# Two more V tiles beside each chain are loaded as two halves

## The chip, the cores and the metric

The kernel runs on one core of a Trainium2 chip. The metric is the device time of one execution in microseconds (us), as the median of several runs; lower is better.

## The reference, cut to what matters

The program computes a decode step: 8 sequences (B), one token each (width D = 448), two layers of attention over a cached K and V, each followed by a small mixer and MLP block. Both layers use the same weights and the same cache.

```python
def _A_ref(x, k_cache, v_cache, wq, wo):          # B 8, Hq 16, Hkv 8, Sk 4096, Dh 256
    q = (x @ wq).reshape(B, Sq, Hq, Dh).transpose(0, 2, 1, 3)
    k = jnp.repeat(k_cache, 2, axis=1)
    v = jnp.repeat(v_cache, 2, axis=1)
    scores = jnp.einsum("bhqd,bhkd->bhqk", q, k) * (Dh ** -0.5)
    o = jnp.einsum("bhqk,bhkd->bhqd", _softmax(scores), v)
    return o.transpose(0, 2, 1, 3).reshape(B, Sq, Hq * Dh) @ wo

x = A_x
x = x + _A_ref(_layernorm(x), K, V, wq, wo)
x = x + _B_ref(_layernorm(x), w1, w2, w3, w4)     # ends in gelu(layernorm(x1) @ w3) @ w4
x = x + _A_ref(_layernorm(x), K, V, wq, wo)
x = x + _B_ref(_layernorm(x), w1, w2, w3, w4)
```

With one token, the shifts of the mixer move zeros in, so that the kernel needs only `w3` and `w4` of block B. K and V are 8 x 8 x 4096 x 256 values of bf16 each, 134 MB apiece; together, and twice, that is nearly all that the kernel reads.

## The kernel before, in words

**Tiles and tasks.** A task is one layer (`ps` 0 or 1), one sequence `b` and one of four pairs of K/V heads (`gp`). Its K and its V come in four tiles of 1 MB each, 128 partitions by 4096 values (8 KB a partition). A K tile is transposed in blocks by DVE (L779) and multiplied with the queries on PE (L794); ACT takes the exponential (L803). A V tile is multiplied with the probabilities on PE (`pv`, L847): 16 matmuls, each over 256 of the 4096 columns, in column order, with room for a step of other work between the eighth and the ninth where the caller asks for it. All tiles live in 15 places of SBUF (`places`, `slots`). Part of one sequence's tiles stay in their places from the first layer to the second and are not loaded again.

**The chain.** The second layer of a sequence can start only when its first layer is through all four pairs. That needs a string of small dependent steps, the chain: scale and turn the output (`half`, L477), multiply by `wo` (L365), normalise (L227 to L302, a sum over partitions on PE at L235, a power on POOL at L254), `w3` (L383), gelu, `w4` (L365), normalise again, `wq` (L316), and spread the query (L335, L339). There is one chain for each of the 8 sequences. The steps are Python generators; `step` lets them go on a little between the tiles, so that PE's instructions for a chain and those for V tiles alternate in one order that is fixed when the program is built.

**The order around a chain.** `first_kept` lays out the work of a sequence. The V tiles that are to be worked off beside the chain are collected in `due`: those of three or four tasks that were scored before. All of them go into `narrow`; for a narrow V, `pv` lets the chain step between its two halves of eight matmuls. Up to 11 of them (`AFTER`) are put directly behind the last V's of the sequence, and the rest are spread over what follows. In the text, "first V", "second V" and "third V" are `due[0]`, `due[1]` and `due[2]`, and their order on PE is that order.

**The loads.** SP issues all K and V loads, in the order in which the tiles are used (`emit_loads`), as soon as a place is free in that order. A place is free when PE or DVE has finished with what is in it. A tile in `halved` is loaded by two transfers of 512 KB (L769: columns 0 to 2047, then 2048 to 4095); any other by one of 1 MB (L766), and pairs of K tiles by one of 2 MB (L741). The matmuls of `pv` wait for the transfer that writes the columns which they read, and a transfer into a place waits for the matmuls that read the columns which it overwrites, so halves are waited for and released as halves. Beside a chain only three places take part: the first, second and third V have one each, the fourth uses the first V's, the fifth the second's, and so on.

Before the change, `halved` holds `due[2]` up to `due[n + 1]`, with `n` the number of V's put behind the last V's of the sequence (11, or 10 in the later chains). `due[0]` and `due[1]` are loaded whole.

Of the kernel before, what the change touches and what calls it, by code (L numbers as in the profile page):

```python
# [17 lines left out]
def kernel(  # L18
# [545 lines left out]
    tasks, items, due = [], [], []  # L564
    number, narrow, halved, loose = {}, set(), set(), set()
    AFTER = 11

    def block(k, v=None):

        fresh = [(number[v], 1, c) for c in range(4)] if v else []  # L570
        if k is None:
            due.extend(fresh)
            items.extend(due)
            due.clear()
            return
        number[k] = len(tasks)
        tasks.append(k)
        two = k[0] == 1 and k[2] in keep
        for c in range(4):
            items.append((number[k], 0, c))  # L580
            if two and c % 2 == 0:
                continue
            items.extend(due[:1])
            del due[:1]
            if c <= two:
                due.extend(fresh)

    def first_kept(b, units, before):

        k2, k3 = ((0, b, gp) for gp in keep)  # L590
        todo = list(units)
        block(todo.pop(0), before)
        if len(todo) > 2:
            block(todo.pop(0))
        block(k2)
        block(todo.pop(0), k2)
        if todo:
            block(todo.pop(0))
        assert not todo
        block(k3)  # L600
        block(None, k3)
        for u in units:
            due.extend((number[u], 1, c) for c in range(4))
        n = min(AFTER, len(due) - 2)
        narrow.update(due)
        if n == AFTER:
            loose.update(due)
        halved.update(due[2 : n + 2])
        items.extend(due[:n])
        del due[:n]  # L610

    block((0, 0, free[0]))
    block((0, 0, free[1]), (0, 0, free[0]))
    first_kept(0, ahead[0], (0, 0, free[1]))
    for b in range(Bn):
        k3, k2 = ((1, b, gp) for gp in keep[::-1])
        block(k3)
        block(k2, k3)
        if b + 1 < Bn:
            first_kept(b + 1, ahead[b + 1], k2)  # L620
        else:
            block((1, b, free[0]), k2)
            block((1, b, free[1]), (1, b, free[0]))
            block(None, (1, b, free[1]))
# [336 lines left out]
    for idx, it in enumerate(items):  # L961
# [7 lines left out]
        n, kv, c = it  # L969
# [202 lines left out]
```

## Time and profile before

| What | Value |
|---|---|
| Median of 3 runs | 1088.32 us (1086.39 to 1088.36) |
| The profiled execution | 1085.17 us, span 1083.3 us |
| Moved by DMA | 438.22 MB, mean 405 GB/s |
| K and V loads on SP | 65 of 2 MB, 62 + 123 of 1 MB, 170 of 512 KB, 8 of 768 KB |
| PE, DVE, ACT busy | 61%, 56%, 15% |

The profiled execution's own time stands beside its span: 1.87 us lie around the span. "L847" is a line of the kernel; `o<-places,ptw` names what an instruction writes and reads. PE is TensorE, PEld its weight loads, DVE VectorE, ACT ScalarE, POOL GpSimd; SPq is the sequencer of SyncE, which issues loads. "Landing" is the moment when the last part of a transfer has reported that it is done. The first row of loads for each chain stands in SP's timeline like this one, of the first chain (start, length from the first issue to the last, what, count):

```profile
149.50 32.45 SPq L769 DMA_DIRECT2D places<-in_A_v_cache_dram  x22
```

The eight chains begin with such rows at 149.50, 280.18, 409.48, 539.02, 657.43, 767.46, 877.55 and 988.17 us.

### The profile page before, as it was taken

To read this page: it belongs to the slowest core of one execution; us is meant where nothing else is said; L and a number is where in the kernel's file an instruction comes from. 1 tells how busy PE (TensorE), PEld (TensorE's weight loads), DVE (VectorE), ACT (ScalarE), POOL (GpSimd) and SP (SyncE) were. 2 spreads that over 40 slices of the span, in tenths; PEclk is the share of its full clock that TensorE was granted. 3 is DMA by queue.
4 is the path that set the end of the run, shared out by engine and by line. 5 is a ranking of instruction groups with operands and counts; after the bars stand their busy time and mean duration, and the time that the engine had idled before them with its cause. 6 is when DMAs were issued, how large, how long until landed. Compare 5 with 4: busy or idle time off the path is not lost.

```text
span 1083.3 us, 29794 instructions
## 1 busy us (share of the span) xinstructions
PE 655.5 (61%) x13292; PEld 411.6 (38%) x13292; DVE 610.5 (56%) x1266; ACT 161.9 (15%) x612; POOL 16.4 (2%) x27
## 2 busy tenths in 40 slices
PE   3244458644776447764486547754785468756775
PEld 2122235422443224532254324532453245433554
DVE  4357841677326872368625773297329743874271
ACT  0001111111111111111112111111111111111110
POOL 0000000000000000000000000000000000000000
PEclk9985555655565555655556555655566556655565
DMA  9999999999999999999999999999999999999994
GB/s 360 394 425 427 425 394 390 423 424 424 394 411 423 428 420 379 415 426 422 421 388 420 423 423 389 388 424 426 405 384 426 424 384 400 426 423 405 394 420 182
DMA packets 66896, 438.22 MB, mean 405 GB/s; under 512 B 7112, under 2 KB 11088, under 8 KB 34384
## 3 DMA queue, kind: packets, MB, share of 16 engines
q1 hardware_dynamic: 66576, 435.94, 98.4%
q8 instruction: 104, 1.70, 0.6%
q10 hardware_dynamic: 192, 0.38, 0.1%
q14 instruction: 24, 0.20, 0.0%
HBM read 436.28 MB, written 0.01 MB: 403 GB/s over the span
## 4 chain that ended last, share of the span: by engine, by line
DMA 60%; PE 19%; DVE 14%; SPq 3%; issue 2%; ACT 1%; POOL 1%; DVEq 0%; ACTq 0%
DMA places<-in_A_v_cache_dram 30%; DMA places<-in_A_k_cache_dram 29%; DVE places L779 9%; PE sc L794 6%; PE o L847 5%; PE misc L365 2%; SPq L174 2%; PE misc L383 1%; PE misc L316 1%; PE misc L477 1%; SPq L766 1%; DVE places L821 1%; DMA wq_sb<-in_A_wq_dram 1%; POOL t L254 1%; DVE qbd L339 1%
## 5 line engine op out<-in xcount | busy, mean ns | idle before, releaser
L779 DVE STREAM_TRANSPOSE places<-places 128x512 uint32<-128x512 uint32 (+1 forms) x576 | 458.0, 855 | 126.0 <-DMA places<-in_A_k_cache_dram 123.7
L794 PE MATMUL sc<-places,qbd 128*8 128x256 bf16 (+1 forms) x4896 | 246.9, 352 | 241.9 <-DVE places L779 234.4
L847 PE MATMUL o<-places,ptw 128*8 128x256 bf16 x3968 | 250.1, 387 | 114.2 <-DMA places<-in_A_v_cache_dram 93.2
L794 PEld LDWEIGHTS <-qbd 128*8 128x8 bf16 x4896 | 129.4, 104 | 324.6 <-DVE places L779 145.3
L847 PEld LDWEIGHTS <-ptw 128*8 128x8 bf16 x3968 | 101.0, 102 | 178.3 <-issue 96.1
L803 ACT ACTIVATE p_n<-sc 128x256 bf16<-128x256 f32 x128 | 95.0, 742 | 382.9 <-PE sc L794 382.9
L957 ACT COPY ptw<-psv 128x32 bf16<-128x32 bf16 x248 | 52.4, 225 | 202.3 <-PE o L847 187.2
L837 ACT CAST psv<-misc 128x128 bf16<-128x128 f32 x64 | 17.1, 267 | 233.7 <-PE misc L830 233.7
L441 DVE RECIPROCAL rz<-misc 128x8 f32<-128x8 f32 (+1 forms) x35 | 6.6, 189 | 70.2 <-PE misc L438 70.2
L316 PEld LDWEIGHTS <-wq_sb 128*128 128x128 bf16 x1152 | 34.2, 104 | 28.0 <-issue 18.1
L365 PEld LDWEIGHTS <-wo_sb 128*128 128x128 bf16 x1280 | 38.1, 103 | 16.4 <-issue 16.2
L339 DVE CAST qbd<-misc 32x64 bf16<-32x64 f32 x104 | 22.4, 215 | 30.9 <-PE misc L335 29.9
L477 PE MATMUL misc<-R_t,o_sb 128*128 128x8 f32 (+1 forms) x132 | 28.6, 326 | 13.4 <-ACT o_sb L471 7.1
L316 PE MATMUL misc<-xb,wq_sb 128*128 128x1 bf16 x1024 | 33.3, 166 | 4.5 <-issue 2.8
L477 PEld LDWEIGHTS misc<-R_t,o_sb 128*128 128x128 f32 x132 | 25.7, 272 | 24.4 <-ACT o_sb L471 14.0
L803 ACT ACTIVATION_READ_ACCUMULATOR p_n<-sc 128x1 f32 x128 | 33.5, 262 | 0.0
L365 PE MATMUL misc<-OT,wo_sb 128*128 128x1 bf16 x1024 | 31.8, 165 | 2.0 <-DVE OT L481 1.7
L473 DVE MEMSET o<- 128x256 f32 x33 | 9.0, 272 | 39.6 <-PE o L847 37.0
L325 DVE CAST qT<-misc 128x32 bf16<-128x32 f32 x8 | 1.5, 192 | 52.7 <-PE misc L316 52.7
L254 POOL TENSOR_TENSOR t<-t,nhalf 128x2 f32<-128x2 f32 (+2 forms) x20 | 14.0, 705 | 1054.7 <-DVE t L275 1054.7
L383 PE MATMUL misc<-xb,w_sb 128*128 128x1 bf16 (+1 forms) x560 | 19.1, 166 | 10.5 <-DVE xb L283 6.4
L383 PEld LDWEIGHTS <-w_sb 128*128 128x128 bf16 x560 | 18.1, 105 | 18.6 <-issue 17.8
(107 smaller groups left out, 306.9 us busy)
## 6 DMA issues: line engine op xcount, KB each, us to landing
places<-in_A_k_cache_dram SPq DMA_DIRECT2D x65, 2048.0 KB, 19.3
places<-in_A_v_cache_dram SPq DMA_DIRECT2D x123, 1024.0 KB, 21.1
places<-in_A_v_cache_dram SPq DMA_DIRECT2D x170, 512.0 KB, 6.7
places<-in_A_k_cache_dram SPq DMA_DIRECT2D x62, 1024.0 KB, 16.1
places<-in_A_v_cache_dram SPq DMA_DIRECT2D x8, 768.0 KB, 6.8
wo_sb<-in_A_wo_dram SPq DMA_DIRECT2D x1, 3584.0 KB, 27.5
wq_sb<-in_A_wq_dram SPq DMA_DIRECT2D x3, 1024.0 KB, 9.0
w_sb<-in_B_w_dram SPq DMA_DIRECT2D x1, 1568.0 KB
```

Source lines behind the costliest of these rows:

```text
L174: nc.sync.dma_start(t[:, fc * cols : (fc + 1) * cols], src[fc * 128 : fc * 128 + 128, :])
L254: nc.gpsimd.tensor_tensor(rs[:, k0:k1].rearrange("p n b -> p (n b)"), ve[:, k0:k1].rearrange("p n b -> p (n b)"), nhalf[:].to_broadcast([1 ...
L316: nc.tensor.matmul(q_ps[:, j * Hq + h, :], w, xbs(nb)[:, xi, :], start=(fc == 0), stop=(fc == 3),)
L339: nc.vector.tensor_copy(qbd[32 * a : 32 * a + 32, :, :, a, :], qs.rearrange("p e (f g u h) -> p (e f) u g h", f=2, u=2, h=2)[:, :, u],)
L365: nc.tensor.matmul(y_ps[:, fc, :], w[:, i, at : at + 128], rhs(i), start=start, stop=stop, skip_group_check=open is not None,)
L383: nc.tensor.matmul(h_ps[:, c * nb : c * nb + nb], w, xbs(nb)[:, xi, :], start=(fc == 0), stop=(fc == 3),)
L477: nc.tensor.matmul(ot_ps[:, j], o_sb[:].rearrange("p (i j) -> p j i", j=2)[:, j], R, start=True, stop=True)
L779: nc.vector.transpose(w, w)
L794: nc.tensor.matmul(sc[32 * k : 32 * k + 8, 128 * x : 128 * (x + nx)], qbd[:, ep, gp].rearrange("p a h -> p (a h)"), v, start=(n == 0), sto ...
L803: nc.scalar.activation(p_sb[:, :, :, 2 * u : 2 * u + 2].rearrange("p t i x -> p x t i"), sc[:, 256 * u : 256 * u + 256].rearrange("p (x t ...
L847: nc.tensor.matmul(o_ps[32 * q : 32 * q + 8, :], ptz[:, at : at + 8], v[:, y * Dh : (y + 1) * Dh], start=False, stop=(y >= 12), skip_group ...
L957: nc.scalar.copy(ptw[:, ring_of[it], :, 6:8], psv[slot_of[it[0]]][:, it[2]])
```

## The change

`halved` begins with `due[0]`: the first and the second V beside each chain are loaded as two transfers of 512 KB each, as the ones after them already are. Nothing else is changed. In the program's order of instructions, SP has 16 more transfers: before each of the eight chains, the last two of the whole V loads become four halves (22 halves in a row become 26 in the first four chains, 20 become 24 in the last four). PE, DVE, ACT and POOL have the same instructions in the same order.

```diff
@@ -605,7 +605,7 @@
         narrow.update(due)
         if n == AFTER:
             loose.update(due)
-        halved.update(due[2 : n + 2])
+        halved.update(due[: n + 2])
         items.extend(due[:n])
         del due[:n]
 
```

## The prediction

> **What bounds the kernel now.** I read the page's first lines, then the chain of work that ended last, then three stretches in the view by windows, then one chain step by step (V's and chains as named in the section on the kernel).
>
> From the page:
>
> ```profile
> PE 655.5 (61%) x13292; PEld 411.6 (38%) x13292; DVE 610.5 (56%) x1266; ACT 161.9 (15%) x612; POOL 16.4 (2%) x27
> ...
> q1 hardware_dynamic: 66576, 435.94, 98.4%
> q8 instruction: 104, 1.70, 0.6%
> ...
> DMA 60%; PE 19%; DVE 14%; SPq 3%; issue 2%; ACT 1%; POOL 1%; DVEq 0%; ACTq 0%
> ```
>
> No engine is over 61% busy; the load queue is at 98.4%, and 60% of the chain is DMA. The kernel is bound by loads, so a change counts if it lets the loads run closer to their full rate. By windows (length, busy of PE, PEld, DVE, ACT, POOL, granted clock, DMA share, GB/s), one stretch before and one inside each of the first two chains:
>
> ```profile
> 122.00:147.00 25.00, 10.93 (x212) 5.59 (x202) 19.70 (x25) 3.54 (x11) 0.00 (x0) 0.50 1.01 422
> 157.00:167.00 10.00, 8.76 (x196) 5.58 (x189) 2.69 (x16) 0.98 (x5) 0.71 (x1) 0.50 0.95 322
> 253.00:278.00 25.00, 10.18 (x196) 5.07 (x184) 19.70 (x25) 3.38 (x12) 0.00 (x0) 0.50 1.01 422
> 287.00:297.00 10.00, 9.02 (x216) 6.14 (x217) 2.62 (x15) 1.15 (x6) 0.70 (x1) 0.50 0.99 358
> ```
>
> Beside a chain the loads fall from 422 GB/s to 322 and 358. Why, the first chain shows. PE's timeline (start, length, what, idle time before it and what ended it):
>
> ```profile
> 152.73 1.03 PE L847 MATMUL o<-places,ptw 128*8 128x256 bf16 x16 [0.51 <-DMA places<-in_A_v_cache_dram]
> 155.31 0.60 PE L847 MATMUL o<-places,ptw 128*8 128x256 bf16 x8 [1.55 <-DMA places<-in_A_v_cache_dram]
> 155.84 1.02 PE L477 MATMUL misc<-R_t,o_sb 128*128 128x8 f32 x4
> 156.79 0.60 PE L847 MATMUL o<-places,ptw 128*8 128x256 bf16 x8
> ...
> 159.74 1.03 PE L847 MATMUL o<-places,ptw 128*8 128x256 bf16 x16
> 160.69 0.59 PE L235 MATMUL misc<-t,one 128*128 128x2 f32 x2
> 161.21 1.03 PE L847 MATMUL o<-places,ptw 128*8 128x256 bf16 x16
> ```
>
> The x8 at 155.31 is the first half of the first narrow V; it waited for the whole megabyte, though its eight matmuls read only the first 512 KB. The chain of waits has that load and a later one:
>
> ```profile
> 132.51 22.67 DMA places<-in_A_v_cache_dram
> 155.18 0.14 issue
> 155.31 0.60 PE o L847 x8
> 155.91 0.95 PE misc L477 x4
> ...
> 165.44 0.56 PE o L847 x8
> 166.00 0.02 issue
> 166.02 7.69 DMA places<-in_A_v_cache_dram
> ```
>
> The first narrow V lands at 132.51 + 22.67 = 155.18. The loads behind it wait for PE to free a place: SP issues the third V's halves at 149.50 and 149.93, then nothing until the first V's halves are used, at 155.95 and 157.44. Six microseconds without an issue, with about 3 MB in the queue at 150, run the queue low, and 157 to 167 is where the rate falls. In total PE waits for V loads:
>
> ```profile
> PE o L847 <- DMA places<-in_A_v_cache_dram: 93.2, 72, 6.1
> ```
>
> **The change, part by part.** The order of instructions on PE, DVE, ACT and POOL does not move. On SP, two whole V loads (L766) before each of eight chains become four halves (L769): 16 more transfers, no more bytes.
>
> *Removed: the wait of the first narrow V.* Halves in line land 1.25 us apart (the third V's at 158.91 and 160.16), so the first half of the first V should land at about 153.95 instead of 155.18. PE ends the V before at 153.76, so it starts at about 154.07: 1.24 earlier. In the eight chains the wait there is 1.55, 1.00, 1.03, 1.44, 1.15, 1.40, 1.56 and 0.98; capped at 1.24 that is 9.1 us. What is late next in chain 1: L477, whose operand ACT has ready at 154.2, then the second half, landing at 155.2; both move along. The second narrow V is halved too, so its first half is there (156.4) when PE comes at about 157.0.
>
> *What of it reaches the loads.* The bound is the queue, so what counts is how much closer together the loads land. The issues at 155.95, 157.44, 158.90 and 160.38 come 1.0 to 1.25 earlier. The first of them gains nothing: it lands at 161.41, in line (second V 157.66, then three halves at 1.25). PE needs it in the second half of the x16 at 161.21, so there PE loses most of its lead. The next lands at 163.64, 2.23 after it: a hole of 0.98 that an earlier issue can fill; two further on is one of 0.37. Taking in each chain the lateness over 1.25 of those early halves that landed within 6.9 us of their issue (little queued before them), capped at the gap that PE loses, I get 1.20, 0.93, 1.03, 0.78, 1.15, 1.24, 1.24 and 0.96: 8.5 us, the most. The least: part of a hole is a code transfer on one of the 16 DMA engines (0.6% of 16 times 1083.3 over 104 packets is 1.0 us each), which stays. In chain 1 the late half took 6.20 from issue to landing where the one before it took 5.46, so some 0.75 of its lateness is not lack of issue; 0.75 off eight holes leaves 2.5 us. Between 2.5 and 8.5 nothing in the trace decides; I take half of the upper end, **4.3 us**. It carries to the end if the loads stay the bound after the chain; they do by the windows (422 GB/s until the next chain).
>
> *Added: transfers.* Whole V's in line land 2.48 apart, halves 1.25 in the same place (2.50 a pair: +0.02) and up to 1.28 later in a chain (+0.08). For 16 V's that is 0.3 to 1.3 us on the bound queue; I take **0.8 us**. Against that stands a rule: the Trainium skill, page "DMA: Bandwidth & Descriptors", section "Bandwidth", wants transfers of at least 1 MiB for 75% of peak, and its section "Anatomy of one DMA" gives a fixed cost of about 2.0 us each, both for DMAs that GpSimd issues. If that fixed cost were paid in line, 16 more transfers would be 32 us and the time about 1117 (an estimate from that page). The rows above differ: 512 KB in 1.25 us is 419 GB/s, so the cost is overlapped.
>
> *SP's queue.* Each extra issue takes 0.33 to 0.42 us on SP, 0.8 a chain, in the 15 us between the last V issue (134.79) and 149.50, where SP waits for PE. The program also makes each load wait for the landing of the load eight before it. The second V's second half then waits for a K load that lands at 141.53, 7.97 before SP's next issue at 149.50; in all chains that margin is 7.9 or more. If the cover went, the third V's halves behind it would be late by what is over. Bound: 0, no gain or loss.
>
> *Waits added:* PE waits for two landings for each of these V's. The second half stands before L365, but lands no later than the whole did, within 0.02 to 0.08. Counted above.
>
> **Sum:** -4.3 + 0.8 = -3.5 us, from the profiled execution's 1085.17 (span 1083.3, 1.87 around it) to 1081.7. That execution is 3.15 (0.29%) under the median of the three runs, 1088.32; on the median the sum is **1084.8**, -0.32%. A measurement can tell about 0.2%, 2.2 us, from no change.
>
> **The rivals.**
>
> *All the lead is kept:* the holes are only lack of issue. -8.5 + 0.3 gives 1080.1. For it: the shares of 0.95 and 0.99 with GB/s down by a quarter and a seventh. Against: the half in line at 161.41, and the code transfers.
>
> *The lead is given back:* PE waits at the next load instead, holes stay. 0 + 0.8 gives 1089.1, within 0.2%. For it: that same half in line. Against: holes after it whose loads are issued behind PE's first two halves.
>
> *Slower: halves are the cause of the low rate, not late issue.* Place: the first 10 us of each chain, where the 4 KB rows take over. At 358 GB/s a megabyte takes 2.93 instead of 2.48; 16 times 0.45 is +7.2, less any gain: 1095.5 at worst. It decides from 0.14 us an extra transfer (2.2 over 16) with no gain, 0.36 with the gain of 4.3. For it: the DMA share stays near 1 while the rate falls. Against: halves in line land 1.25 to 1.28 apart.
>
> **How the numbers follow.** Forecast (1 to 6 us gained): 0.42, of it a seventh under 2.2; its own range is 1082.3 to 1087.3. All kept: 0.15. Given back (1 gained to 2.2 lost): 0.25, of it 0.02 over the bound with the spread of runs. Slower: 0.18. Faster by over 0.2%: 0.36 + 0.15 = 0.51; within 0.06 + 0.23 = 0.29; slower 0.20. The range 1080.0 to 1091.0 takes in the two bounds of the gain and the milder half of the slower case; it leaves out about 0.07 below and 0.1 above.
>
> **What would show it.** Right: the first x8 of each chain starts 1.0 to 1.25 sooner after the V before it, the wait for V loads at L847 falls by several us, the rate in the first 10 us of a chain rises, the 512 KB loads number 202. The gain's size is wrong if the rate there stays near 322 and 358 (lead given back); the mechanism is wrong if it falls, or if the 512 KB loads that follow each other land clearly over 1.28 apart. A second V's second half that SP issues after 149.5 would break the SP step.

## The result and the profile after

| | Median (lowest to highest) | Runs |
|---|---|---|
| Before | 1086.75 us (1083.64 to 1088.36) | 6 |
| After | 1079.62 us (1078.85 to 1081.69) | 6 |

The ratio of after to before is 0.9937, with a 95% interval of 0.992 to 0.9954: the change saves 6.8 us, 5.0 to 8.7. Measured twice more in the study it gave 0.9945 (0.9927 to 0.9962) and 0.9937 (0.9915 to 0.996). The forecast was 3.5 us and 1084.8; the measured median lies 0.4 us below the low end of the range. The sign was right, and the mechanism too as far as the runs below show it; the size was half of what came.

The page of the changed kernel shows that little else moved: the same bytes on the load queue, the same busy shares within a point, 2304 more packets on the load queue (144 for each of the 16 extra transfers), the same 104 code transfers (the row of q8).

```profile
PE 654.5 (61%) x13292; PEld 407.1 (38%) x13292; DVE 610.2 (57%) x1266; ACT 162.2 (15%) x612; POOL 16.3 (2%) x27
...
q1 hardware_dynamic: 68880, 435.94, 98.6%
q8 instruction: 104, 1.70, 0.6%
...
DMA 62%; PE 20%; DVE 11%; SPq 2%; issue 2%; ACT 2%; POOL 0%; DVEq 0%; ACTq 0%
```

PE's timeline at the first chain of the changed kernel (start, length, what, idle time before it and what ended it):

```profile
152.94 1.02 PE L847 MATMUL o<-places,ptw 128*8 128x256 bf16 x16 [0.45 <-DMA places<-in_A_v_cache_dram]
154.43 0.60 PE L847 MATMUL o<-places,ptw 128*8 128x256 bf16 x8 [0.47 <-ACT o_sb L471]
154.96 1.02 PE L477 MATMUL misc<-R_t,o_sb 128*128 128x8 f32 x4
155.91 0.60 PE L847 MATMUL o<-places,ptw 128*8 128x256 bf16 x8
...
160.55 0.60 PE L847 MATMUL o<-places,ptw 128*8 128x256 bf16 x8
161.81 0.60 PE L847 MATMUL o<-places,ptw 128*8 128x256 bf16 x8 [0.66 <-DMA places<-in_A_v_cache_dram]
```

The first V no longer waits for a load. It waits 0.47 us for ACT, which copies the finished output to `o_sb`; before, it waited 1.55. And at 161.81, the first half of the fourth V, a wait for a load has come that was not there before. The chain of waits of the same stretch shows both:

```profile
130.89 22.00 DMA places<-in_A_v_cache_dram
152.89 0.04 issue
152.94 1.05 PE o L847 x13
153.99 0.02 issue
154.01 0.38 ACT o_sb L471
154.39 0.04 issue
154.43 0.62 PE o L847 x8
155.06 0.02 issue
155.07 6.70 DMA places<-in_A_v_cache_dram
```

The load that decided before was the whole first V. Now it is the V before it, and the path goes on through the load issued at 155.07, when the first half of the first V's place came free. That issue was at 155.95 before.

So PE's waits for V loads at L847 hardly fall (93.2 us before): what PE gains at the first V it spends a few tiles later, waiting for the loads.

```profile
PE o L847 <- DMA places<-in_A_v_cache_dram: 92.1, 82, 6.0
...
PE o L847 <- ACT o_sb L471: 5.9, 12, 0.6
```

The gain stands in the rate of the loads. I take ten microseconds of each chain, from 7.5 us after SP issued the third V's first half; the first two chains by windows (length, busy of PE, PEld, DVE, ACT, POOL, granted clock, DMA share, GB/s), before:

```profile
157.00:167.00 10.00, 8.76 (x196) 5.58 (x189) 2.69 (x16) 0.98 (x5) 0.71 (x1) 0.50 0.95 322
287.70:297.70 10.00, 9.02 (x201) 5.71 (x198) 2.62 (x15) 0.98 (x5) 0.70 (x1) 0.50 0.99 361
```

and the changed kernel, in its first profile and then in the second of three (e5 below):

```profile
157.30:167.30 10.00, 8.80 (x196) 5.38 (x193) 2.62 (x15) 0.98 (x5) 0.71 (x1) 0.50 0.99 362
287.20:297.20 10.00, 7.32 (x159) 4.48 (x155) 2.62 (x15) 0.98 (x5) 0.70 (x1) 0.53 0.97 354
157.10:167.10 10.00, 8.68 (x200) 5.52 (x197) 2.62 (x15) 0.98 (x5) 0.71 (x1) 0.50 1.01 382
286.70:296.70 10.00, 8.25 (x178) 4.97 (x176) 2.63 (x15) 0.98 (x5) 0.70 (x1) 0.50 1.03 395
```

Single chains scatter: in the first profile the second chain's rate is a little under that of before. Over the eight chains the mean is 352 GB/s before, and 378, 376 and 381 in the three profiles of the changed kernel.

### The profile page after: what moved, and what is told of

Its sections match the earlier page's. It is cut to its first block, busy times and chain, and to the rows that moved or that the text cites. A ratio compares the mean times of both kernels' runs of the same rounds, so it can differ in the third digit from the quotient of the medians.

```text
span 1079.8 us, 29813 instructions
## 1 busy us (share of the span) xinstructions
PE 654.5 (61%) x13292; PEld 407.1 (38%) x13292; DVE 610.2 (57%) x1266; ACT 162.2 (15%) x612; POOL 16.3 (2%) x27
## 4 chain that ended last, share of the span: by engine, by line
DMA 62%; PE 20%; DVE 11%; SPq 2%; issue 2%; ACT 2%; POOL 0%; DVEq 0%; ACTq 0%
DMA places<-in_A_v_cache_dram 35%; DMA places<-in_A_k_cache_dram 24%; PE o L847 7%; DVE places L779 7%; PE sc L794 6%; PE misc L365 2%; SPq L174 2%; PE misc L316 1%; DMA w_sb<-in_B_w_dram 1%; DVE store L814 1%; ACT p_n L803 1%; PE misc L477 1%; PE misc L383 1%; DVE places L821 1%; DMA wq_sb<-in_A_wq_dram 1%
## 5 line engine op out<-in xcount | busy, mean ns | idle before, releaser
L847 PE MATMUL o<-places,ptw 128*8 128x256 bf16 x3968 | 252.1, 386 | 116.5 <-DMA places<-in_A_v_cache_dram 92.1
L847 PEld LDWEIGHTS <-ptw 128*8 128x8 bf16 x3968 | 100.3, 101 | 184.7 <-issue 112.2
L477 PE MATMUL misc<-R_t,o_sb 128*128 128x8 f32 (+1 forms) x132 | 25.9, 305 | 13.4 <-ACT o_sb L471 7.1
L477 PEld LDWEIGHTS misc<-R_t,o_sb 128*128 128x128 f32 x132 | 23.0, 245 | 24.4 <-ACT o_sb L471 14.2
L830 PEld LDWEIGHTS <-p_n 128*128 128x128 bf16 x256 | 11.8, 105 | 31.5 <-issue 20.4
L830 PE MATMUL misc<-identb,p_n 128*128 128x32 bf16 x256 | 18.1, 191 | 8.1 <-ACT p_n L803 6.8
## 6 DMA issues: line engine op xcount, KB each, us to landing
places<-in_A_k_cache_dram SPq DMA_DIRECT2D x62, 1024.0 KB, 13.2
```

Source lines behind the costliest of these rows:

```text
L477: nc.tensor.matmul(ot_ps[:, j], o_sb[:].rearrange("p (i j) -> p j i", j=2)[:, j], R, start=True, stop=True)
L830: nc.tensor.matmul(pt_ps[:, t], p_sb[:, t].rearrange("p i x -> p (i x)"), cols, start=True, stop=True,)
L847: nc.tensor.matmul(o_ps[32 * q : 32 * q + 8, :], ptz[:, at : at + 8], v[:, y * Dh : (y + 1) * Dh], start=False, stop=(y >= 12), skip_group ...
```

## The experiments

Theory A is the prediction's mechanism: places come free sooner, SP issues the following loads sooner, the queue does not run low. Rival T: what counts is how early the chain's own small steps run on PE. Rival C: the second V matters as much as the first. The slower rival, that halves are themselves costly, is refuted by the result as far as the total goes; what halves cost was still to be measured. Gains in us below are ratios times 1087.

**e1: only the first V halved as well.**

```diff
-        halved.update(due[2 : n + 2])
+        halved.update(due[:1] + due[2 : n + 2])
```

> Only the first V beside each chain is halved as well (8 more transfers than before). Theory A (the prediction's mechanism: the lead of PE at the first V brings loads forward; each extra transfer costs little): nearly the whole gain of the full change, which was 7.1 us by medians: 6 to 7.5 us less than before. Rival C (the second V matters as much as the first): about half, 3 to 4 us less.

Measured: 0.9957 (0.9942 to 0.9972), 4.7 us less than before (3.0 to 6.3). That is two thirds of the gain. The interval holds the 3 to 4 us of rival C and only the low end of theory A's 6 to 7.5, so that this run alone does not decide between them. PE's timeline at its first chain shows a wait that the full change does not have:

```profile
154.88 0.60 PE L847 MATMUL o<-places,ptw 128*8 128x256 bf16 x8 [0.47 <-ACT o_sb L471]
...
156.36 0.60 PE L847 MATMUL o<-places,ptw 128*8 128x256 bf16 x8
156.89 1.01 PE L365 MATMUL misc<-OT,wo_sb 128*128 128x1 bf16 x32
158.42 0.60 PE L847 MATMUL o<-places,ptw 128*8 128x256 bf16 x8 [0.52 <-DMA places<-in_A_v_cache_dram]
```

The x8 at 158.42 is the whole second V, which PE now reaches before it has landed. Over the eight chains PE waits for it 0.52, 1.05, 1.10, 0.13, 0.21, 0.86, 1.13 and 0.07 us, 5.1 in all, where before it was 0.7. The stall has moved on by one tile.

**e2: only the second V halved as well.**

```diff
-        halved.update(due[2 : n + 2])
+        halved.update(due[1 : n + 2])
```

> Only the second V beside each chain is halved as well. Theory A: PE waited for the second V in four chains only, 0.14 to 0.19 us each, so 0.7 us less at most, minus the cost of 8 transfers (0.2 to 0.7 us): within 1 us of before. Rival C: 3 to 4 us less than before.

Measured: 0.9985 (0.997 to 1.0), 1.6 us less (0.0 to 3.3). That is hardly told from no change, and the 3 to 4 of rival C lie at the interval's upper end or above it. That halving the second V keeps the lead behind a halved first V is seen in PE's waits of e1; the times do not show it, since 4.7 and 1.6 add up to 6.3, near the whole gain.

**e3: the cost of 16 more transfers by itself.** The first two V's stay whole; the two middle ones of the four V's ahead of them are halved.

```diff
+        halved.update((number[k3], 1, c) for c in (1, 2))
         halved.update(due[2 : n + 2])
```

> The cost of 16 more transfers by itself: the first two V's stay whole as before; instead the two middle ones of the four V's just ahead of them are loaded in halves (they land before PE needs them, but for the release of their places nothing hangs on them). Prediction's term: 0.3 to 1.3 us more than before, 0.8 taken. If the term was oversized: 0 to 0.3 us more, no change that can be measured. Rival (halves cause the low rate): about 7 us more.

Measured: 1.0008 (0.9994 to 1.0023), 0.9 us more, between 0.7 less and 2.5 more. The term of 0.8 lies inside that interval; the 7 us of the slower rival lie outside it. These halves land ahead of the chain, so that the price of a half inside the chain is not measured here. The rate in its chains, with 16 more transfers and no sooner release of places, is not better than before (mean of eight 334 GB/s):

```profile
157.30:167.30 10.00, 8.82 (x195) 5.56 (x194) 2.79 (x16) 0.98 (x5) 0.71 (x1) 0.50 0.95 308
288.50:298.50 10.00, 8.56 (x186) 5.40 (x182) 2.62 (x15) 0.98 (x5) 0.70 (x1) 0.50 0.98 347
```

**e4: full change, and the chain's first step placed later.** `step` is left out behind the last V ahead of the first narrow one, so that the copy to `o_sb` is recorded between the halves of the first V.

```diff
-        step(idx, it in narrow)
+        if not (it[1] and soon[1] and soon in narrow and it not in narrow):
+            step(idx, it in narrow)
```

> The full change, and in addition the copy of the finished output to o_sb, the first step of a chain, is put between the two halves of the first V and not ahead of them. In the changed kernel PE waited 0.48 us for that copy before the first V in each chain. Now the first V's halves can be used at once (up to 0.48 us earlier, 3.8 us over 8 chains), and the chain itself starts about 0.5 us later. Theory A (what counts is when places come free and loads are issued): 1 to 4 us less than the full change, so 8 to 11 us less than before. Rival T (what counts is how early the chain's own steps run on PE): 2 to 4 us more than the full change, so 3 to 5 us less than before.

Measured: 0.9916 (0.99 to 0.9931), 9.1 us less than before (7.5 to 10.9). The chain's steps start later and the kernel is not slower than the full change, against rival T. Counted from SP's issue of the third V's first half, L477 starts after 5.52 us on average over the eight chains, where it is 4.37 to 4.74 in the three profiles of the changed kernel and 5.26 before. So the steps are no earlier than before, and the gain is there; what is early as in the changed kernel is the issue into the first V's place, after 4.41 us, against 4.49 to 4.85 there and 5.37 before. PE's timeline at its first chain: both halves of the first V now wait for their loads and stand ahead of L477, which starts at 156.06 instead of 154.96.

```profile
154.25 0.60 PE L847 MATMUL o<-places,ptw 128*8 128x256 bf16 x8 [0.26 <-DMA places<-in_A_v_cache_dram]
155.53 0.60 PE L847 MATMUL o<-places,ptw 128*8 128x256 bf16 x8 [0.68 <-DMA places<-in_A_v_cache_dram]
156.06 1.02 PE L477 MATMUL misc<-R_t,o_sb 128*128 128x8 f32 x4
```

**e5: the changed kernel again.**

> The changed kernel once more, beside the next two on the same chip, for a second profile and a narrower interval. All theories: 6 to 8 us less than before. Theory A: in this profile too the rate in the first ten microseconds of the chains is above that of before by 5 to 10%.

Measured: 0.9945 (0.9927 to 0.9962), 6.0 us less. The rate in its chains is 376 GB/s against 352, 7% more.

**e6: the later copy without the change** (e4's edit on the kernel before).

> The kernel before, whole first and second V, with only the later place of the copy to o_sb: the first V's two halves of matmuls stand next to each other on PE, ahead of the chain's first step. Theory A: the first V's first place half is released no earlier than before, the second about 1 us earlier (it no longer stands behind L477): 0 to 3 us less than before. Rival T: the chain's own steps start 0.5 to 1 us later in each of 8 chains: 3 to 6 us more than before.

Measured: 1.0003 (0.9986 to 1.0021), 0.3 us more, between 1.5 less and 2.3 more. The chain starts later (L477 after 6.03 us, against 5.26 before, counted as in e4) at no cost that shows: rival T's 3 to 6 us are excluded. Theory A's 0 to 3 us less are neither seen nor excluded; the first half still waits for the whole V there.

**e7: e4 and one more V halved**, the last whole one ahead of the first.

```diff
-        halved.update(due[: n + 2])
+        halved.update([(number[k3], 1, 3)] + due[: n + 2])
```

> The kernel of e4 (full change and later copy), with the last whole V ahead of the first one halved too (8 more transfers). PE waited for that V in the first chain only (0.45 us). Theory A: at most 0.4 us of gain, 0.4 us of cost: the same as e4 within 1 us, 8 to 10 us less than before. If it is faster than e4 by over 2 us, halves help in a way that PE's waits don't show.

Measured: 0.9936 (0.9918 to 0.9955), 7.0 us less, where 8 to 10 were expected; median 1079.45, e4's was 1079.43. No further gain.

**e8 and e9: e4 and the changed kernel side by side.**

> The kernel of e4 again, on one chip with the changed kernel of e9, since e4 and e7 (7 to 9 us less than before) did not stand clear of the change itself (6 to 7 us less). Theory A: 1 to 3 us less than e9, since the first V's halves are used 0.48 us sooner in each chain; at least 1 us less would also be needed to call it a better kernel. Rival T: not less than e9.

> The changed kernel for the third time, to stand beside e8: 6 to 7 us less than before. Theory A, from the two profiles of it so far: the lateness of the landings beside the chains sums to 11 to 14 us in its profile too, against 17 to 22 us in the four profiles with a whole first V.

Measured: e8 0.9933 (0.9907 to 0.9959), e9 0.9937 (0.9915 to 0.996), medians 1079.27 and 1080.25. The intervals overlap almost wholly, so the 1 to 3 us between them that theory A expected are not shown. In three measurements each, kernels with the later copy gave 9.1, 7.0 and 7.3 us and the change alone 6.8, 6.0 and 6.8; a further gain of about 1 us is possible but not shown. The lateness in e9's profile is 10.6 us, a little under the 11 to 14 expected.

**All profiles together.** The lateness of a chain's halves is what their landings, from the trace's completion times, lie further apart than 1.26 us, where that is over 0.1; summed over eight chains, from the landing just before the third V's halves on, 168 halves in all. It is split in two. A half counts as issued late when its turn, 1.26 us after the landing before it, comes less than 5.9 us after its own issue: before the change, no half here landed sooner than 5.1 us after its issue. Beside it stands the mean rate of the eight windows defined above:

| Kernel (one profile each) | Lateness, us | of it, halves issued late (how many) | the others | GB/s | Span, us |
|---|---|---|---|---|---|
| before | 16.8 | 10.3 (33) | 6.5 | 352 | 1083.3 |
| e3, first V whole | 22.0 | 11.9 (38) | 10.1 | 334 | 1088.3 |
| e6, first V whole | 19.8 | 9.8 (43) | 10.0 | 349 | 1088.1 |
| e2, first V whole | 20.4 | 13.8 (33) | 6.6 | 340 | 1086.7 |
| e1, first V halved | 16.3 | 5.7 (23) | 10.6 | 361 | 1083.2 |
| after, e5, e9 | 13.2, 11.1, 10.6 | 1.0 (9), 2.3 (6), 2.1 (13) | 12.2, 8.8, 8.4 | 378, 376, 381 | 1079.8, 1080.2, 1078.9 |
| e4, e8, e7 | 10.1, 7.7, 8.4 | 0.5 (2), 0.2 (3), 0.0 (2) | 9.6, 7.5, 8.4 | 387, 395, 394 | 1079.2, 1075.9, 1079.1 |

Span less lateness is 1066.3 to 1070.7 in all eleven, while the spans differ by 12.4: most of the difference is what the landings beside the chains are late. Four profiles with a whole first V have 19.8 us on average, three of the changed kernel 11.6, about 8.1 less. The split says where: halves issued late are 33 to 43 with a whole first V and 6 to 13 in the changed kernel, and their lateness falls from 9.8 to 13.8 us to 1.0 to 2.3. That of the others does not fall. With a limit of 5.6 or 6.2 in place of 5.9 the picture is the same. This is the prediction's mechanism, seen directly.

Code transfers have a part in the late landings. Of the 17 halves that landed over 0.5 us late before, 14 (13.0 us) have a code transfer that ended within the 2.6 us before their landing; of the 143 on time (late by 0.1 at most), 49 have one. In the three profiles of the changed kernel it is 10 of 12, 8 of 8 and 7 of 8 (9.6, 6.5 and 7.2 us). The stretches hold as many code transfers as before, 34 against 33, 32 and 34. So a large hole is mostly met together with a code transfer, and in the changed kernel fewer of the transfers go with one. No run varies the code transfers, so how the two act together is not shown.

## Why the prediction was right or wrong

**Right: the bound, the place and the sign.** The loads bound the kernel, the queue ran low beside each chain (at 150 us in the first, 4 MB of loads had yet to land, part of it already moved, where the prediction says about 3), and halving the two V's raised the rate there (344 GB/s on average over the four profiles with a whole first V, 378 over the three after). That earlier issue is the cause and not the chain's earlier steps is shown by e4, whose steps are no earlier than before and which has the gain, and by the split above: what went is the lateness of halves issued late. e6, which delays the steps at no loss, agrees.

**Right: the cost of the transfers.** 0.8 us taken, 0.9 measured in e3. The interval there also holds nothing and twice the term, so that the close agreement is in part luck. The Trainium skill gives on its page "DMA: Bandwidth & Descriptors", in the section "Anatomy of one DMA", a fixed cost of about 2.0 us for each transfer that GpSimd issues. On SP's queue it does not show as time in line: 0.9 us over 16 transfers is 0.06 each.

**Right: SP's queue.** In the changed kernel's first chain SP issues the second V's second half at 141.86 and the third V's first half at 149.77, 7.91 later; in all eight chains that margin is 7.9, as forecast.

**Wrong by size: the lead at the first V.** 9.1 us were taken from the landings. PE's wait there fell from 10.1 us in eight chains to 3.9, by 6.2. What the prediction missed is the next wait in line, 0.47 to 0.53 us in each chain for ACT's copy to `o_sb`. The prediction had ACT's copy, but only as an operand of L477. The rows above show the first V's first matmul waiting for it too. In the program both output banks are halves of one tile; that this is the reason is argued, not tested. SP's issue into the first V's place came 0.5 to 0.9 us earlier (4.49 to 4.85 us after the third V's first half, against 5.37), not the 1.0 to 1.25 of the prediction. In e4, where that first matmul no longer waits for the copy, it came after 4.41 us, hardly earlier: PE then waits for the halves themselves, so the copy alone cost the loads little.

**Wrong, and the step that failed: "Between 2.5 and 8.5 nothing in the trace decides; I take half of the upper end".** This is the term of 4.3 us for what reaches the loads, and it was mis-sized: the gross gain is 6.8 + 0.9 = 7.7 us, if the 0.9 of e3 holds. The lateness of halves issued late, which is what the prediction wanted to price, fell from 10.3 us in the profile that it read to 1.8 on average, by 8.5. So the upper end was right, and this with a smaller lead than assumed; that it is 8.5 to the digit is luck. Two things in that step were wrong.

First, 0.75 us of each hole, 6.0 in all, was put down to a code transfer and taken to stay; after that the upper end was halved without a row that says so. The transfers stay, most of that lateness does not. By the DMA view of 159 to 163 us, one code transfer falls into that stretch in both kernels. Before:

```profile
DMA packets 316, 1.15 MB, mean 287 GB/s; under 512 B 39, under 2 KB 39, under 8 KB 315
...
q8 instruction: 1, 0.02, 1.5%
```

After:

```profile
DMA packets 401, 1.48 MB, mean 370 GB/s; under 512 B 43, under 2 KB 43, under 8 KB 400
...
q8 instruction: 1, 0.02, 1.7%
```

Before, a half landed 0.98 us late about then; after, the halves from 161.77 to 168.06 landed within 0.03 us of their turn. The very next half, at 170.56, landed 1.24 us late, with a code transfer that ended at 168.88, and so did others (1.26 us at 293.02, 1.22 at 667.97). So the transfers are not shown to be free; how much of a hole is theirs stays open.

Second, the holes were sized from one profile of before, and a favourable one: 16.8 us of lateness, and a time 3.15 us under the median of that day, while the three other profiles with a whole first V have 19.8 to 22.0. From that profile's own 16.8 the whole lateness falls by only 5.2. The other 2.9 of the 8.1 come from the three other profiles, mostly from halves issued in time, whose lateness scatters from 6.5 to 12.2 us between profiles.

**The base.** Of the 5.2 us between 1084.8 and 1079.62, 1.6 come from the median of before (1088.32 in three runs, 1086.75 in six) and 3.6 from the gain.

**The second V.** The prediction counted on its first half being there when PE comes, and gave that no price. In e1, without it, 5.1 us of waits come back and the gain is 4.7 instead of 6 to 7; the intervals overlap in part.

**The signs listed there.** The first x8 was to start 1.0 to 1.25 sooner after the V before it. It did in two chains (1.08 in the first); in the others it was 0.5 to 0.96, with about 0.5 where the old wait was 1.0. 512 KB loads are 202. The rate rose. That the wait for V loads at L847 would fall by several us was a poor sign: it is 92.1, 87.1 and 85.6 in three profiles against 93.2, since PE's waits moved to later tiles, as at 161.81. A sign that was not listed is the shortest time from issue to landing of a half in the first chain; before, as minimum, median and longest:

```profile
DMA to landing us min/median/max: 5.5/6.8/10.2
```

and after:

```profile
DMA to landing us min/median/max: 6.5/7.0/10.3
```

No half in this view lands as quickly as 5.5 us any more. Over the eight chains these minima are 5.2 to 5.8 before and 5.5 to 6.8 after, which fits halves that have more ahead of them in the queue.

## What to carry to other kernels

Where loads are the bound and few places circulate, the worth of a consumer's earlier start is the queue time that its earlier releases fill, not the wait that it loses; count the late landings, not PE's waits. When a wait at one tile is removed, look at the very next tile and at every operand of the next instruction: here they took 5.1 us (e1) and 3.9 us (the copy) of PE's waits. And a bound of that kind should be summed from several executions, since four profiles with a whole first V had from 16.8 to 22.0 us of lateness.

## What the runs showed of the hardware that was not expected

Splitting a 1 MB load of 128 rows into two of 512 KB on SP's queue cost 0.06 us a transfer (e3, 0.9 us over 16, not told from zero). Beside the chains of the kernel before, no half landed sooner than 5.1 us after its issue, against 1.25 us between landings in a full queue. The 24 of 168 halves whose turn came less than 5.6 us after their issue carry 9.0 of the 16.8 us of lateness. So a load had to be issued about four transfers ahead of its turn, which fits the cost of six microseconds without an issue.

The same kernel's runs spread more than the change is worth: before ranged from 1082.59 to 1090.74 us in 23 runs beside each other, so that the later copy's extra microsecond could not be settled with six runs.
